# Total of three groups: sums in the off-diagonal quadrants, interleaved with the next group's scores, and copied in two halves

## The chip, the cores and the metric

The kernel runs on one core of a Trainium2 chip. The metric is the time of one execution in device microseconds (us); the kernel before took 373.97 us, the median of 3 runs (372.93 to 374.14). The times of single instructions below come from one profiled execution.

## The reference

For each of 4 batches and 8 heads, a state of 64x64 decays by a factor of its head at each of 768 steps and takes up one outer product; the output is the query times that state:

```python
for t in range(S):
    state = gamma * state + einsum('bhd,bhe->bhde', k[:, :, t], v[:, :, t])
    y[:, :, t] = scale * einsum('bhd,bhde->bhe', q[:, :, t], state)
```

The heads' outputs side by side are `x` (768 x 512 per batch), and go through a gated layer: `h = relu(x @ w_in)` is cut into `u` and `v`; `v` is normalised over its columns, multiplied by `w_spatial` over the steps, a bias is added, and `(u * v_s) @ w_out` is the output.

## The kernel before, in words

**Groups.** The steps of a batch are cut into 6 groups of 128 steps (24 groups in all), a group into two halves `i` of 64 steps. The 8 heads are 4 pairs `hp` of 2 heads `r`. The two heads of a pair lie in partitions 0 to 63 and 64 to 127; `place(hp, r)` says which (the order alternates with `hp`). Decay is taken out by scaling: values are multiplied beforehand (`scale_values`, "p"), outputs afterwards (`out_evict`, "E"), so the state is a plain running sum. For each half a head has three kinds of products of 64x64x64: its scores (keys times queries, `score`, "q"), masked on VectorE (`ret_mask`, "j"); its part of the state (`naturals` times `values`); and its outputs (`out_products`, "y"), which take the masked scores and the state before the half. Each of these float32 products is recorded as two matmuls, so a group has 32 for scores, 16 for each half's state, 32 for each half's outputs.

**Quadrants.** A product of 64x64 uses a quarter of TensorE's array: the input's partitions choose the rows, the output's partitions the columns. `score` reads and writes the same 64 partitions: diagonal quadrants.

**The state in the first groups.** Groups 0 to 5 (batch 0) run in an opening whose order is written out by hand in the string `START`; its words are a letter and a number, emitted in order, and each engine keeps that order. There the state is kept as one total in PSUM: `total_sum(g, i)`, word `t`, adds the half's products to the tile `total` (L301 to L314), in the diagonal quadrants. `total_copy(g, i)`, word `k`, has ScalarE copy the whole tile into the state that the next half's outputs read (L316 to L318). The next sum may not write before that copy has read. Eleven sums and copies are made, `t00` to `t50`.

**The other stages.** After the opening, `ret_set` (L340 to L375) interleaves scores of the next group with state products whose output goes to the other 64 partitions; there a copy or an addition per 64 partitions brings them back.

**Other words of `START` that the change passes.** `V` is the product of `x` with the `v` half of `w_in` (large matmuls of 128x128x512, three per word), `h` and `l` split a group's output `x` into a high and a low part (ScalarE, then GpSimd or VectorE), `a`, `c`, `H` and `R` split a weight from 64-bit words into high and low parts (ScalarE, VectorE, ScalarE, then GpSimd or VectorE), `r`, `s`, `w`, `n` and `N` normalise. `G` and `L` and `K` are loads on SyncE's queue: a group's keys and queries (`qk`, 3 buffers) and values (`vk`, 2 buffers), a weight, a part of `w_spatial`. A group's load waits until the outputs of the group three earlier are done.

**After the opening** the order of TensorE's work is written out too (`FIRST`, `REST`, `LAST`); the order on the other engines is made by the framework's own planner.

Of the kernel before, what the change touches and what calls it, by code (L numbers as in the profile page):

```python
# [21 lines left out]


START = (
# [10 lines left out]
)  # L35
FIRST = (
    "S6 W0 I4 W1 D1 X6 J9 S7 G9 D2 I5 X7 J10 G10 D3 W2 S8 W3 I6 X8 S9 V0 G11 W4 I7 X9 J11 S10 "
# [24 lines left out]
def tile_retention_gmlp(  # L62
# [12 lines left out]
    nc = tc.nc  # L75
    P = 128
    B = out.shape[0]
# [12 lines left out]
    ROWS = [slice(0, D), slice(D, P)]  # L90
# [27 lines left out]
    def keep(ins):  # L118

        if fixed:  # L120
            tc.keep_in_program_order(ins)

    def mm(out, lhs, rhs, start, stop, pin=False, shared=False):
        ins = nc.tensor.matmul(out, lhs, rhs, start=start, stop=stop, skip_group_check=shared)  # L124
        if pin or pinned or fixed:
            tc.keep_in_program_order(ins)
# [32 lines left out]
    def slot(n, dtype, name):  # L159

        cols = HALF // 2 if dtype == I64 else HALF
        return mpool.tile([P, HC, cols], dtype, tag=f"sp{n}", name=name, bufs=1)
# [5 lines left out]
    for n in ROOMS:  # L168
        t = slot(n, F32, f"room{n}").rearrange("p s c -> p (s c)")
# [85 lines left out]
    def place(hp, r):  # L255

        return ROWS[(r + hp) % 2]
# [40 lines left out]
    total = {}  # L298
    marks = {}

    def total_sum(g, i):  # L301
        if not total:
            total[0] = ps_o.tile([P, NP, D], F32, tag="o", name="total")
        for hp in range(NP):
            for r in range(2):
                rows = place(hp, r)
                mm(
                    total[0][rows, hp],
                    naturals[g][rows, i, hp],
                    values[g][rows, i, hp],  # L310
                    start=(g == 0 and i == 0 and hp == 0),
                    stop=True,
                    shared=True,
                )  # L314

    def total_copy(g, i):  # L316
        dst = states[g][:, 1] if i == 0 else states[g + 1][:, 0]
        keep(nc.scalar.copy(dst, total[0]))  # L318

    def score(g, i, hp, r, pin=False):  # L320
        rows = place(hp, r)
        ops = keys[g][rows, i, hp], queries[g][rows, i, hp]
        mm(marks[g][rows, i, hp], *ops, start=True, stop=True, pin=pin)

    def bank(name):
        return ps_r.tile([P, 2, NP, C], F32, tag="ret", name=name)
# [8 lines left out]
    def ret_mask(g):  # L335
        mk = mask_t[:, :].unsqueeze(1).broadcast_to([P, 2 * NP, C])
        s, d = (t.rearrange("p i h c -> p (i h) c") for t in (marks.pop(g), scores[g]))
        keep(nc.vector.tensor_tensor(d, s, mk, ALU.mult))
# [360 lines left out]
    def decay_copy():  # L699
# [17 lines left out]
        "q": lambda b, g, n: ret_scores(n),  # L717
        "p": lambda b, g, n: scale_values(n % 10, pick(n // 10)),
        "j": lambda b, g, n: ret_mask(n),
        "t": lambda b, g, n: total_sum(n // 10, n % 10),  # L720
        "k": lambda b, g, n: total_copy(n // 10, n % 10),
        "y": lambda b, g, n: out_products(n // 10, n % 10),
        "E": lambda b, g, n: out_evict(n),
# [114 lines left out]
```

## Time and profile before

| | us |
|---|---|
| median of 3 runs | 373.97 |
| the profiled execution's own time | 374.42 |
| its span in the trace | 372.7 |
| TensorE busy | 362.0 (97%) |
| VectorE busy | 237.2 (64%) |
| ScalarE busy | 155.1 (42%) |
| GpSimd busy | 135.5 (36%) |

The granted clock of TensorE is full (1.00) over the span. The span runs from the first to the last instruction; the execution's own time has 1.7 us around it. Engines are named PE (TensorE's matmuls), PEld (its weight loads), DVE (VectorE), ACT (ScalarE), POOL (GpSimd) and SP (SyncE). Matmuls are recorded with modelled ends and overlap, so a group's span is from its first start to the last one's end.

### The profile page before, as it was taken

How to read it: one execution, taken by the hardware profiler on the slowest of the kernel's cores; microseconds unless marked ns; L12 is line 12 of the kernel's file. 1: busy time of each engine (PE TensorE's matmuls, PEld its weight loads, DVE VectorE, ACT ScalarE, POOL GpSimd, SP SyncE). 2: the span in 40 equal slices, each digit the busy share in tenths (PEclk: the TensorE clock that was granted, in tenths of full speed). 3: DMA queues.
4: the chain of work that ended last, by engine and by line, in shares of the span. 5: the costliest groups of instructions: out<-in, count | busy, mean ns of one | idle time of the engine just before them, and what ended most of it. 6: DMA issues, size and time to landing. Idle time of an engine off the chain costs nothing.

```text
span 372.7 us, 10303 instructions
## 1 busy us (share of the span) xinstructions
PE 362.0 (97%) x4420; PEld 316.6 (85%) x4420; DVE 237.2 (64%) x514; ACT 155.1 (42%) x309; POOL 135.5 (36%) x137
## 2 busy tenths in 40 slices
PE   7798999999999999999999999999999999999995
PEld 3687785797998879999998888999998888999984
DVE  4989979995887866677674543376774433165530
ACT  3595781274334545533114445432323445432232
POOL 2254750001353523526424451327424341325041
PEclk9999999999999999999999999999999999999999
DMA  7997773001331731113305332021404002000022
GB/s 262 413 365 261 272 300 130 0 2 63 138 114 58 253 115 64 61 55 112 118 2 199 114 114 86 8 106 52 179 1 141 3 2 86 0 0 2 0 87 84
DMA packets 13153, 41.20 MB, mean 111 GB/s; under 512 B 1586, under 2 KB 1842, under 8 KB 13108
## 3 DMA queue, kind: packets, MB, share of 16 engines
q1 hardware_dynamic: 12964, 40.42, 29.8%
q8 instruction: 35, 0.57, 0.7%
q10 hardware_dynamic: 144, 0.13, 0.1%
q14 instruction: 10, 0.08, 0.1%
HBM read 34.25 MB, written 6.29 MB: 109 GB/s over the span
## 4 chain that ended last, share of the span: by engine, by line
PE 94%; DMA 2%; DVE 1%; issue 1%; ACT 0%; SPq 0%; POOL 0%; POOLq 0%; DVEq 0%
PE u L124 18%; PE v L124 18%; PE o L124 18%; PE y L124 10%; PE sp L124 8%; PE x L124 7%; PE z L124 5%; PE s L124 3%; PE d L124 3%; PE w L124 3%; DMA decay_t<-in_decay_dram 2%; PE total L124 1%; PE o_last L124 0%; SPq L129 0%; DVE xf L417 0%
## 5 line engine op out<-in xcount | busy, mean ns | idle before, releaser
L124 PE MATMUL u<-xh,winu_w 128*128 128x384 f32 x256 | 68.1, 338 | 0.0
L124 PE MATMUL v<-winv_w,xh 128*128 128x512 f32 x192 | 60.6, 397 | 0.0
L124 PE MATMUL o<-wout_w,gh 128*128 128x512 f32 (+1 forms) x192 | 60.4, 396 | 0.0
L124 PEld LDWEIGHTS u<-xh,winu_w 128*128 128x128 f32 x256 | 46.5, 188 | 0.8
L132 POOL TENSOR_TENSOR xl<-xf,xh 128x512 fp32r<-128x512 f32 x21 | 29.4, 1398 | 37.3 <-ACT xh L434 37.3
L124 PE MATMUL u<-xl,winu_w 128*128 128x384 f32 x128 | 42.9, 335 | 0.0
L124 PEld LDWEIGHTS v<-winv_w,xh 128*128 128x128 f32 x192 | 35.2, 188 | 7.8
L124 PE MATMUL y<-sp,a 128*128 128x384 f32 x216 | 41.6, 336 | 0.0
L124 PEld LDWEIGHTS o<-wout_w,gh 128*128 128x128 f32 x192 | 35.2, 188 | 7.3
L532 ACT CAST a<-vn 128x384 fp32r<-128x384 f32 x42 | 21.6, 514 | 46.0 <-PE y L124 16.9
L132 DVE TENSOR_TENSOR a<-vn,a 128x384 fp32r<-128x384 f32 x42 | 24.9, 593 | 24.6 <-ACT a L532 24.2
L132 POOL TENSOR_TENSOR gl<-ur,gh 128x384 fp32r<-128x384 f32 x24 | 26.8, 1116 | 37.4 <-ACT gh L628 37.0
L124 PEld LDWEIGHTS y<-sp,a 128*128 128x128 f32 x216 | 38.0, 188 | 0.2
L124 PE MATMUL v<-winv_w,xl 128*128 128x512 f32 x96 | 37.5, 390 | 0.0
L124 PE MATMUL o<-wout_w,gl 128*128 128x512 f32 (+1 forms) x96 | 37.3, 389 | 0.0
L475 DVE BATCH_NORM_STATS2 bst<-vr 128x6 f32<-128x512 f32 x24 | 16.6, 691 | 28.6 <-ACT vr L468 28.6
L417 DVE SCALAR_TENSOR_TENSOR xf<-x,decay_t,qd_t 128x128 f32<-128x128 f32 x96 | 27.1, 343 | 10.3 <-PE x L124 9.7
L482 POOL TENSOR_TENSOR rs<-rs,mhalf 128x1 f32<-128x1 f32 x24 | 13.5, 566 | 42.6 <-DVE rs L477 42.1
L124 PE MATMUL s<-qk 64*64 64x64 f32 x768 | 27.4, 221 | 0.1
L124 PEld LDWEIGHTS s<-qk 64*64 64x64 f32 x768 | 25.2, 137 | 2.1 <-issue 1.1
L498 ACT ACTIVATE vn<-vr,nb,rs 128x512 f32<-128x512 f32 x24 | 19.4, 814 | 17.8 <-DVE nb L487 16.8
L593 ACT ACTIVATE ur<-u 128x384 f32<-128x384 f32 x32 | 15.7, 490 | 26.8 <-PE u L124 26.6
(111 smaller groups left out, 671.7 us busy)
## 6 DMA issues: line engine op xcount, KB each, us to landing
qk<-in_groups_dram SPq DMA_DIRECT2D x24, 512.0 KB, 5.4
vk<-in_groups_dram SPq DMA_DIRECT2D x21, 512.0 KB, 4.8
out_dram<-ot SPq DMA_DIRECT2D x23, 256.0 KB, 2.9
wst<-in_w_sp_dram SPq DMA_DIRECT2D x4, 576.0 KB, 7.9
raw<-in_w_inv_dram SPq DMA_DIRECT2D x4, 512.0 KB, 7.3
raw<-in_w_inu_dram SPq DMA_DIRECT2D x4, 512.0 KB, 7.0
raw<-in_w_out_dram SPq DMA_DIRECT2D x4, 512.0 KB, 5.2
third<-in_groups_dram SPq DMA_DIRECT2D x3, 512.0 KB, 7.4
```

The source lines that it names most:

```text
L124: ins = nc.tensor.matmul(out, lhs, rhs, start=start, stop=stop, skip_group_check=shared)
L132: return eng.tensor_tensor(out, whole, high.bitcast(F32), ALU.subtract)
L417: nc.vector.scalar_tensor_tensor(xf[:, hp], t[hp % 2][:, hp // 2].rearrange("p i c -> p (i c)"), qg_t[:, c, hp : hp + 1], qd_t[:, hp], ALU ...
L475: keep(nc.vector.bn_stats(st, norm[b, c][0]))
L482: keep(nc.gpsimd.tensor_tensor(rs, rs, mhalf, ALU.pow))
L498: keep(nc.scalar.activation(vn[b][:, c], v, AF.Identity, bias=nb, scale=rs))
L532: nc.scalar.copy(t[:, 0], whole)
L593: keep(nc.scalar.activation(u, pu[:, :HALF], AF.Relu))
```

## The change

In the opening, the scores of groups 3, 4 and 5 are no longer a block of their own ahead of the sums (`q3`, `q4`, `q5`). `total_sum` of groups 2, 3 and 4 makes them: with `with_scores` each product of the sum follows one score of the next group, half `i` with half `i`. In `START` these sums have a 1 in front (`t120`, `t121`, `t130` and so on). All sums, also those without scores, now write to the other 64 partitions, so that `total` holds the pair's heads exchanged, and `total_copy` exchanges them back with two copies of 64 partitions. The masks of groups 4 and 5 move: `j4` from behind `h2` to behind `t131`, `j5` from behind `a4` to behind `t141`; `j3` keeps its place. The other words keep their order.

```diff
-    "h0 k01 c21 j1 t10 y10 a1 H2 k10 G3 c10 y11 p22 t11 c22 q2 c11 k11 c12 L3 l0 H1 q3 t20 k20 "
-    "E1 G4 R1 V00 j2 h1 t21 l11 p23 k21 y20 y21 L5 R2 j3 q4 t30 E2 a3 h2 j4 c30 V10 p24 V01 V11 "
-    "V02 L4 l12 c31 V20 a5 k30 y30 c32 t31 H3 k31 c50 G5 y31 q5 E3 t40 a4 j5 R3 V21 V12 k40 c40 "
-    "L6 c51 y40 p25 y41 t41 h3 l3 V03 a6 k41 c41 E4 c42 c52 r0 s0 G6 h4 l4 H4 V22 L8 R4 V13 V23 "
+    "E0 q1 h0 k01 c21 j1 t10 y10 a1 H2 k10 G3 c10 y11 p22 t11 c22 q2 c11 k11 c12 L3 l0 H1 "
+    "t120 k20 E1 G4 R1 V00 j2 h1 t121 l11 p23 k21 y20 y21 L5 R2 j3 t130 E2 a3 h2 c30 V10 p24 "
+    "V01 V11 V02 L4 l12 c31 V20 a5 k30 y30 c32 t131 j4 H3 k31 c50 G5 y31 E3 t140 a4 R3 V21 "
+    "V12 k40 c40 L6 c51 y40 p25 y41 t141 j5 h3 l3 V03 a6 k41 c41 E4 c42 c52 r0 s0 G6 h4 l4 H4 "
...
-    def total_sum(g, i):
+    def total_sum(g, i, with_scores=False):
         if not total:
             total[0] = ps_o.tile([P, NP, D], F32, tag="o", name="total")
+        if with_scores and i == 0:
+            marks[g + 1] = bank(f"s{g + 1}")
         for hp in range(NP):
             for r in range(2):
-                rows = place(hp, r)
+                if with_scores:
+                    score(g + 1, i, hp, r)
+                rows, other = place(hp, r), place(hp, 1 - r)
                 mm(
-                    total[0][rows, hp],
+                    total[0][other, hp],
...
     def total_copy(g, i):
         dst = states[g][:, 1] if i == 0 else states[g + 1][:, 0]
-        keep(nc.scalar.copy(dst, total[0]))
+        for r in range(2):
+            keep(nc.scalar.copy(dst[ROWS[r]], total[0][ROWS[1 - r]]))
...
-        "t": lambda b, g, n: total_sum(n // 10, n % 10),
+        "t": lambda b, g, n: total_sum(n // 10 % 10, n % 10, n >= 100),
```

## Rows read from the trace of the kernel before

**Rows 1.** The page's chain that ended last, by engine.
```profile
PE 94%; DMA 2%; DVE 1%; issue 1%; ACT 0%; SPq 0%; POOL 0%; POOLq 0%; DVEq 0%
```

**Rows 2.** Windows: stretch, its length, busy us and count of each engine, clock, DMA.
```profile
50.00:100.00 50.00, 50.00 (x381) 39.51 (x380) 42.07 (x84) 22.31 (x43) 5.69 (x6) 1.00 0.24 89
...
15.90:31.30 15.40, 13.89 (x381) 12.21 (x382) 13.76 (x26) 11.37 (x36) 8.39 (x6) 1.00 0.90 335
31.30:39.20 7.90, 7.18 (x126) 5.60 (x125) 7.79 (x19) 5.47 (x16) 2.09 (x2) 1.00 0.70 246
```

**Rows 3.** Timeline of PE: start, us, instruction, count, idle before and its releaser.
```profile
16.74 0.28 PE L124 MATMUL x<-ws,vk 64*64 64x64 f32 x3 [0.87 <-issue]
...
17.48 1.97 PE L124 MATMUL s<-qk 64*64 64x64 f32 x62
...
20.81 0.90 PE L124 MATMUL total<-third 64*64 64x64 f32 x15
...
23.46 0.63 PE L124 MATMUL total<-vk 64*64 64x64 f32 x15
...
31.82 0.33 PE L124 MATMUL total<-vk 64*64 64x64 f32 x3 [1.19 <-issue]
...
35.21 0.73 PE L124 MATMUL v<-winv_w,xh 128*128 128x512 f32 x2
...
39.39 0.28 PE L124 MATMUL x<-qk,third 64*64 64x64 f32 x4 [0.39 <-issue]
...
44.59 0.39 PE L124 MATMUL v<-winv_w,xl 128*128 128x512 f32 x1
```

**Rows 4.** DMA, 29.4 to 30.5 us: queue, packets, MB, share of 16 engines.
```profile
q8 instruction: 1, 0.02, 5.9%
```

**Rows 5.** DMA, 37.0 to 38.3 us.
```profile
q8 instruction: 1, 0.02, 5.3%
```

**Rows 6.** DMA, 31 to 37 us.
```profile
q1 hardware_dynamic: 480, 1.80, 87.0%
```

**Rows 7.** Timeline of SyncE's issues: start, us, what.
```profile
29.39 0.33 SPq L129 DMA_DIRECT2D qk<-in_groups_dram  x1
...
31.38 0.42 SPq L129 DMA_DIRECT2D wst<-in_w_sp_dram  x1
```

**Rows 8.** Line L124, 79.6 to 80.75 us: count, ns min/median/max, first and last start.
```profile
L124 PE MATMUL s<-qk x32: 218/218/267, 79.7 to 80.7; 64*64 64x64 f32 x32
...
L124 PE MATMUL d<-vk x32: 218/218/267, 79.8 to 80.7; 64*64 64x64 f32 x32
```

**Rows 9.** ScalarE's groups by form: count, busy us, mean ns, idle before.
```profile
L369 ACT COPY ws<-d 64x256 f32<-64x256 f32 x6 | 2.2, 367 | 0.6 <-PE d L124 0.6
```

**Rows 10.** Timeline of ScalarE.
```profile
18.83 0.35 ACT L318 COPY third<-total 128x256 f32<-128x256 f32 x1
...
20.03 0.37 ACT L318 COPY third<-total 128x256 f32<-128x256 f32 x1 [0.33 <-PE total L124]
...
22.75 0.35 ACT L318 COPY ws<-total 128x256 f32<-128x256 f32 x1
23.00 0.68 ACT L176 ACTIVATE room<-raw 128x512 f32<-128x512 f32 x1
...
28.93 0.37 ACT L318 COPY ws<-total 128x256 f32<-128x256 f32 x1 [0.92 <-PE total L124]
```

**Rows 11.** Timeline of VectorE.
```profile
34.43 0.43 DVE L197 TENSOR_SCALAR room<-df 128x512 int32<-128x512 int32 x1
...
35.49 1.41 DVE L197 TENSOR_SCALAR room<-df 128x512 int32<-128x512 int32 x1
...
41.47 1.12 DVE L417 SCALAR_TENSOR_TENSOR xf<-x,decay_t,qd_t 128x128 f32<-128x128 f32 x4 [0.32 <-PE x L124]
...
43.52 0.68 DVE L132 TENSOR_TENSOR xl<-xf,xh 128x512 fp32r<-128x512 f32 x1
```

**Rows 12.** Timeline of GpSimd.
```profile
35.06 1.55 POOL L132 TENSOR_TENSOR xl<-xf,xh 128x512 fp32r<-128x512 f32 x1 [3.98 <-ACT xh L434]
```

12 rows, old and new, of the table START are left out of this document.

## The prediction

> **What bounds the kernel now.** I began with the chain that ended last: TensorE holds 94% of it and DMA 2% [rows 1]. Then the busy time by stretch: from 50 to 100 us TensorE is busy for all 50.00 us [rows 2]. So whatever moves the moment at which TensorE leaves the opening (about 50 us, where the change lies) moves the end by as much, and nothing else does. Inside the opening TensorE is not full. I read its timeline for idle marked "issue", which means that it waited for nothing that the profile shows: 0.87 us before 16.74, 1.19 before 31.82 and 0.39 before 39.39 [rows 3]. Between the first two gaps lie 382 weight loads, between the last two 125 [rows 2]: that is three times 127, and 127 again. A gap after every 127th pair of weight load and matmul (the boundaries between pass with little or no gap) looks like the instruction stream itself, arriving in blocks. The DMA view says so too: in queue 8, "instruction", one packet of 0.02 MB is under way in 29.4 to 30.5 us [rows 4] and one in 37.0 to 38.3 us [rows 5], and TensorE goes on about 2.4 us after the start of each window, at 31.82 and 39.39. In the six microseconds before, 31 to 37, the load queue alone is listed, at 87.0% of all 16 DMA engines, and queue 8 moves nothing [rows 6]. The loads that fill this stretch were issued from 29.39 (qk6) to 31.38 (half of the spatial weights) [rows 7]. I read it so: the block that TensorE needs at 39 us is asked for when it takes up the block before, at 31.82, and is served behind the loads issued by then.
>
> The Trainium skill, "Runtime: NRT & Kernel Launch", section "Instruction fetch mechanics", says that the stream comes in blocks of 256 instructions of 16 KiB, fetched while the block before runs, and that the cost of crossing is mostly hidden. Size and count agree with rows 2, 4 and 5; the hiding does not, in this opening, where the three gaps add up to 2.45 us [rows 3]. By that rule the 2.0 us worked out below would pass on, as in the first rival.
>
> **The change part by part.** *Products interleaved.* A group's scores run at 1.97 us for 62 recorded matmuls, less 0.22 for the last one to drain: 28 to 29 ns each [rows 3]. Where scores and state products alternate between the diagonal and the other quadrants, as the later stages already do, 32 and 32 take 0.95 us from first to last start (79.7 to 80.7), 14.5 ns each [rows 8]. Each of the three groups has 32 score and 32 total matmuls, so 64 x 14.5 ns = 0.93 us is saved per group, 2.8 us in all, as far as TensorE is free to run them.
>
> *Copies in halves.* A copy of 64x256 takes 0.37 us on the mean [rows 9], and one of 128x256 0.35 to 0.37 us [rows 10], so a half costs what the whole did; the one after it starts 0.25 to 0.27 us later (22.75 to 23.00 [rows 10]). Eleven more copies are 2.9 us of ScalarE, and each total copy ends 0.26 us later.
>
> Now stage by stage, because most of both is hidden.
>
> To 16.74 us: the copies of groups 0 and 1 stand in the chain (the next sum may not overwrite the total before both halves have read it). Three of them follow one another before the gap, at most 0.8 us; the gap of 0.87 us [rows 3] hides it, since the block's packet waits for loads that are issued earlier and don't move. Without the gap it would cost the 0.8.
>
> Group 2 (17 to 22 us): the copy of the first total, k20, starts at 20.03 and ends at 20.40 [rows 10]. ScalarE can reach it at 18.83 + 2 x 0.26 + 0.52 (the cast behind k11) = 19.88, and its second half then ends at about 20.5. So t21 with scores starts at 20.55 instead of 20.81 [rows 3], gains 0.26 us at most, and runs into the end of a block in its 30th matmul of 32; the kernel before meets the same boundary in the 14th of its 16 there and ends it late (0.90 us for 15 matmuls [rows 3], against 0.63 at 29 ns). Gain 0.
>
> Group 3 (22 to 24 us): k21 starts at 22.75 and ends at 23.10 [rows 10], and the 0.93 us of scores hid that: t30 starts at 23.46 [rows 3]. Now the first score is followed by a product that must wait for both halves. With 0.12 us that ScalarE is behind, they end at about 23.50; t30 with scores runs to 24.0, where t30 ended. Gain 0, or a loss of 0.05.
>
> Group 4 (29 to 35 us): the same again with k31, which starts at 28.93 [rows 10]; the halves end at 29.56, so t40 with scores runs from 29.6 to 30.1. But now the boundary that cost 1.19 us falls elsewhere: the stream up to it is the same 382 pairs, but six large matmuls (V21, V12) and eight of y40 stand ahead of it. They take 1.5 us and fill the gap; TensorE reaches the boundary at 31.75 and goes on at 31.82 as before. Left are 88 small matmuls (24 of y40, 32 of y41, 32 of t41 with scores) x 14.5 ns = 1.28 us, so the next large ones start at 33.2 instead of 35.21 [rows 3]: 2.0 us ahead.
>
> The next block ends in y50, 125 pairs on, now at about 36.8. Its successor is asked for at 31.82 as before, behind the same loads (qk6 is issued when y31 ends, at most 0.1 us later), and comes at 37.1: TensorE goes on at 39.4 [rows 3, 5]. The 2.0 us become a gap of 2.6 us. I take this value, 0. The bounds: if the block came without waiting, the 2.0 us pass on; if it came later by what its request is later, the loss is that of the second rival.
>
> The Trainium skill, "DMA: Bandwidth & Descriptors", section "Queues, rings and completion order", says that a DMA engine takes turns between its queues packet by packet. Then the instruction packet would pass the waiting loads; rows 6 speak against it. By it the result is again the first rival.
>
> *VectorE.* The masks j4 and j5 move behind the later halves of their scores; both have time before y40 and y50. But VectorE is full here, and its plain tensor_scalar operations stall beside GpSimd: 1.41 us at 35.49 beside GpSimd's operation at 35.06 to 36.61 [rows 11, 12], where one alone takes 0.43 (34.43). Moved work changes which one meets it: I count one such stall lost and one gained, and 0.3 us of lateness from ScalarE's. There is room: VectorE waits 0.32 us for TensorE at 41.47, and the low part of group 5's output at 43.52 (0.68 us long, done at 44.20 [rows 11]) is wanted at 44.59 [rows 3], so 0.39 more. Cost 0 to 0.1; without that cover 0.3, and 1.0 for each further stall.
>
> Sum for the profiled execution: 0 + 0 (to 0.05) + 0 + 0 to 0.1, about +0.1 on its own 374.42 us (span 372.7 and 1.7 around it). It stands 0.45 above the median of 373.97, so I forecast 374.0.
>
> **The rivals.** *The fetch is not tied to the loads.* Then TensorE is 2.0 us ahead at 36.8. For it: the profile puts the gaps down to "issue" and names no load. Against it: rows 6. But the low part at 43.52 caps it: VectorE can be earlier by 0.32 and has 0.39 in hand, so 0.7 us, 373.3, no measurable change; only if VectorE also loses a stall (1.0 us) does 1.7 come through: 372.3.
> *All 2.8 us arrive*: 371.2. For it: the pace of rows 8. Against: the copies that the sums wait for in rows 10.
> *Slower: the fetch comes a fixed time after the boundary.* In the trace the block ends at 30.63 (31.82 less the idle 1.19) and the packet's window opens at 37.0. If that 6.4 us is the fetch's own time and not a queue of loads, the boundary now at 31.75 brings the packet at 38.1 and TensorE back at about 40.5, 1.1 to 1.35 us later: 375.3. It decides as soon as the boundary falls after 30.63, which it does. Against it: the packet of 29.4 [rows 4] came some 2.5 us after its boundary, which by the count of 127 lies in the large matmuls near 27 us.
> *VectorE meets two more stalls*: 0.3 + 2.0 - 0.7 = 1.6 us, 375.6.
>
> **How the numbers follow.** The forecast 0.56; the free fetch 0.16, of it 0.07 with no measurable change; all of the saving 0.06; the fixed fetch 0.15; VectorE's stalls 0.07. A measurement of this kernel can tell 0.3% (1.1 us) from no change. Faster 0.09 + 0.06 = 0.15, same 0.56 + 0.07 = 0.63, slower 0.22. The forecast's own range is 373.3 to 374.8. Left out below is the full saving (0.06), above the far part of the stalls; the range is 372.3 to 375.5.
>
> **What would show it.** Right: a TensorE gap of 2 us or more near 37 to 39.4 us and the restart within 0.2 us of 39.39; no gap near 31; the first large matmuls of 35.21 near 33.2; scores and total together at 14.5 ns. Wrong: the packet of 37.1 moved by more than 0.3 us, either way, or the low part of 43.52 arriving late with TensorE waiting for it. A time below 372.8 or above 375.1 would refute the forecast.

## The result and the profile after

The change makes the kernel slower: 376.76 us, the median of 7 runs (375.76 to 377.29), against 373.97. The ratio on record is 1.0067 (it is not the quotient of the two medians), with an interval of 1.0046 to 1.0088, so 1.7 to 3.3 us. The forecast was 374.0 with a range up to 375.5. The profiled execution took 376.83 us with a span of 375.1, 2.4 us longer than before. Of the experiment e1_halves below, one execution took 902.91 us and is left out.

TensorE holds 90% of the chain that ended last instead of 94% [rows 1]; VectorE and ScalarE have come in.

```profile
PE 90%; DMA 3%; DVE 3%; ACT 2%; issue 1%; SPq 0%; POOL 0%; POOLq 0%
```

By stretch (columns as in [rows 2]), TensorE is again full from 50 to 100 us, and the difference arises in the opening. A stretch at half the granted clock, 1.2 GHz, runs from about 17.7 to 21.1 us; the profiled execution before stood at 1.00 throughout, but 28 of 82 other executions of the kernel before have a mean granted clock of 0.990 to 0.995, so such stretches are not new with the change.

```profile
17.50:18.00 0.50, 0.44 (x10) 0.30 (x14) 0.50 (x2) 0.47 (x3) 0.00 (x0) 0.69 1.00 401
18.00:21.00 3.00, 3.00 (x86) 3.00 (x86) 2.77 (x8) 2.94 (x11) 0.00 (x0) 0.50 0.65 218
21.00:21.50 0.50, 0.50 (x29) 0.43 (x22) 0.50 (x1) 0.17 (x1) 0.26 (x1) 0.90 0.94 344
...
50.00:100.00 50.00, 50.00 (x381) 39.45 (x380) 42.03 (x86) 22.83 (x42) 7.10 (x8) 1.00 0.30 110
```

**The timeline of TensorE after.** It shows where the opening falls behind.

```profile
15.81 0.51 PE L124 MATMUL total<-vk 64*64 64x64 f32 x10 [3.08 <-issue]
...
25.72 0.27 PE L124 MATMUL total<-vk 64*64 64x64 f32 x1 [1.66 <-ACT ws L323]
...
26.34 0.73 PE L124 MATMUL v<-winv_w,xh 128*128 128x512 f32 x2
...
34.53 0.33 PE L124 MATMUL x<-ws,vk 64*64 64x64 f32 x4 [0.18 <-DVE xf L422]
...
36.70 0.73 PE L124 MATMUL v<-winv_w,xh 128*128 128x512 f32 x2
...
40.66 0.27 PE L124 MATMUL x<-third,third 64*64 64x64 f32 x2 [0.18 <-DVE xf L422]
...
43.52 0.72 PE L124 MATMUL v<-winv_w,xh 128*128 128x512 f32 x2
...
51.89 0.33 PE L124 MATMUL u<-xh,winu_w 128*128 128x384 f32 x1
```

The same points of the kernel before, to be set against these:

```profile
24.03 0.73 PE L124 MATMUL v<-winv_w,xh 128*128 128x512 f32 x2
...
41.28 0.73 PE L124 MATMUL v<-winv_w,xh 128*128 128x512 f32 x2
...
49.57 0.33 PE L124 MATMUL u<-xh,winu_w 128*128 128x384 f32 x1
```

The reader is to see three steps. TensorE is 26.34 - 24.03 = 2.31 us late when the large products of group 1 start. At V03, the next large products after group 4's sums (36.70, before 35.21 [rows 3]), it is only 1.49 late: 0.8 us have been won back, by products at the new pace and because the gap of 1.19 us before 31.82 [rows 3] is gone, less new waits of 0.39 us for `k31` and of 0.18 us twice for `E3`. At V30 (43.52 against 41.28) it is 2.24 late again, and that is carried to the end (51.89 against 49.57, +2.32). So something takes time before 26 us, and something else takes the gain back between 36 and 43 us. The lateness before 26 us need not reach the end: the experiment e6_early_half below is 1.42 us late at V10 (25.45) and 0.13 at the `u` products (49.70).

**Before 16 us.** ScalarE's timeline after:

```profile
10.12 0.76 ACT L323 COPY ws<-total 64x256 f32<-64x256 f32 x2 [0.36 <-PE total L124]
10.90 0.68 ACT L176 ACTIVATE room<-raw 128x512 f32<-128x512 f32 x1
14.32 0.62 ACT L439 CAST xh<-xf 128x512 fp32r<-128x512 f32 x1 [2.74 <-DVE xf L422]
14.97 0.74 ACT L323 COPY ws<-total 64x256 f32<-64x256 f32 x2
```

From the start of `k00` to the next instruction, `a2`, it is 0.78 us. A whole copy let the next one start 0.25 to 0.27 us after it [rows 10]. The two halves run one behind the other, 0.39 us each, and cost 0.51 us more instead of the 0.26 of the prediction. VectorE after:

```profile
11.62 0.43 DVE L182 TENSOR_SCALAR room<-room 128x512 f32<-128x512 f32 x1 [1.01 <-ACT room L176]
12.08 1.18 DVE L184 TENSOR_SCALAR room<-room 128x512 int32<-128x512 int32 x1
13.18 1.11 DVE L422 SCALAR_TENSOR_TENSOR xf<-x,decay_t,qd_t 128x128 f32<-128x128 f32 x4
```

and before:

```profile
11.12 0.43 DVE L182 TENSOR_SCALAR room<-room 128x512 f32<-128x512 f32 x1 [0.49 <-ACT room L176]
11.58 0.43 DVE L184 TENSOR_SCALAR room<-room 128x512 int32<-128x512 int32 x1
11.92 1.12 DVE L417 SCALAR_TENSOR_TENSOR xf<-x,decay_t,qd_t 128x128 f32<-128x128 f32 x4
```

Half a microsecond later, L184 runs into GpSimd's scaling of the values of group 1:

```profile
11.93 1.04 POOL L296 TENSOR_TENSOR vk<-vk,decay_t 128x512 f32<-128x512 f32 x1 [2.60 <-DMA vk<-in_groups_dram]
```

It takes 1.18 us instead of 0.43. The first eviction, `E0`, starts 1.26 us later (13.18 against 11.92), `h0` and behind it `k01` follow, and the sum that may not overwrite the total before `k01` has read it, `t10`, starts at 15.81 after 3.08 us of idle TensorE. `k01` ends at 15.71, yet the profile marks this idle time "issue"; the mark alone does not prove that an engine waits for its instructions. In the kernel before, `t10` started here:

```profile
14.07 0.68 PE L124 MATMUL total<-vk 64*64 64x64 f32 x16 [1.54 <-POOL vk L296]
```

The Trainium skill, "SBUF — State Buffer", section "Who interferes with whom", says that a tensor_scalar in a two-port mode and a GpSimd operation lock each other out for a whole instruction; the trace agrees (1.18 against 0.43 us), though it does not show the mode.

**Between 30 and 43 us.** VectorE after:

```profile
31.18 0.69 DVE L343 TENSOR_TENSOR ws<-s,mask_t 128x512 f32<-128x512 f32 x1 [1.12 <-PE total L124]
31.79 0.64 DVE L182 TENSOR_SCALAR room<-room 128x512 f32<-128x512 f32 x1
32.47 1.40 DVE L184 TENSOR_SCALAR room<-room 128x512 int32<-128x512 int32 x1
33.78 1.11 DVE L422 SCALAR_TENSOR_TENSOR xf<-x,decay_t,qd_t 128x128 f32<-128x128 f32 x4
...
39.40 1.12 DVE L422 SCALAR_TENSOR_TENSOR xf<-x,decay_t,qd_t 128x128 f32<-128x128 f32 x4
```

and before:

```profile
23.86 0.68 DVE L338 TENSOR_TENSOR ws<-s,mask_t 128x512 f32<-128x512 f32 x1
...
31.29 1.11 DVE L417 SCALAR_TENSOR_TENSOR xf<-x,decay_t,qd_t 128x128 f32<-128x128 f32 x4
...
36.82 1.11 DVE L417 SCALAR_TENSOR_TENSOR xf<-x,decay_t,qd_t 128x128 f32<-128x128 f32 x4
```

The mask `j4` ran at 23.86 without a wait. Now it stands behind `t131` and VectorE, full before, sits idle for 1.12 us until those scores are there. What is queued behind it, two operations on a weight (the second takes 1.40 us, beside GpSimd's operation of 32.23 to 33.58) and then the eviction `E3`, moves: `E3` starts at 33.78 (+2.49), `E4` at 39.40 (+2.58). TensorE's rows above name `xf L422` at 34.53 and 40.66: `y40` waits for `E3` and `y50` for `E4`, because a group's outputs take the two PSUM tiles that are left beside `total`, and the eviction of the group before frees them. And on ScalarE

```profile
40.55 0.62 ACT L439 CAST xh<-xf 128x512 fp32r<-128x512 f32 x1 [2.25 <-DVE xf L422]
...
42.21 0.76 ACT L323 COPY third<-total 64x256 f32<-64x256 f32 x2
```

`h4`, which waits 2.25 us for `E4`, holds up what stands behind it on ScalarE, and so `k50`, the copy that `y51` needs; then V30 follows, 2.24 us late. The forecast gap near 39.4 us is gone: TensorE has no idle marked "issue" from 26 to 44 us. In the DMA view of 38.2 to 39.0 us the instruction packet is there:

```profile
q8 instruction: 1, 0.02, 7.5%
```

In steps of 0.05 us it begins at 38.45, and before at 37.05 [rows 5]: 1.4 us later. TensorE goes on some 2.4 us behind such a packet (below), which would be about 40.85 here, and it gets there only then, at 40.88: the wait for `E4` hides the gap.

### The profile page after: what moved, and what is told of

Read it like the earlier page. It is cut to its first block, busy times and chain, and to the rows that moved or that the text cites. A ratio compares the mean times of both kernels' runs of the same rounds, so it can differ in the third digit from the quotient of the medians.

```text
span 375.1 us, 10314 instructions
## 1 busy us (share of the span) xinstructions
PE 362.2 (97%) x4420; PEld 316.1 (84%) x4420; DVE 236.8 (63%) x514; ACT 160.5 (43%) x320; POOL 134.8 (36%) x137
## 4 chain that ended last, share of the span: by engine, by line
PE 90%; DMA 3%; DVE 3%; ACT 2%; issue 1%; SPq 0%; POOL 0%; POOLq 0%
PE u L124 18%; PE o L124 18%; PE v L124 17%; PE y L124 10%; PE sp L124 8%; PE x L124 6%; PE z L124 5%; PE d L124 3%; PE s L124 2%; PE w L124 2%; DMA decay_t<-in_decay_dram 2%; DMA qk<-in_groups_dram 1%; PE total L124 1%; ACT ws L323 1%; DVE xf L422 1%
## 5 line engine op out<-in xcount | busy, mean ns | idle before, releaser
L124 PE MATMUL u<-xh,winu_w 128*128 128x384 f32 x256 | 68.2, 338 | 0.0
L124 PE MATMUL v<-winv_w,xh 128*128 128x512 f32 x192 | 60.6, 397 | 0.0
L124 PE MATMUL o<-wout_w,gh 128*128 128x512 f32 (+1 forms) x192 | 60.4, 396 | 0.0
L124 PEld LDWEIGHTS u<-xh,winu_w 128*128 128x128 f32 x256 | 46.5, 188 | 0.8
L132 POOL TENSOR_TENSOR xl<-xf,xh 128x512 fp32r<-128x512 f32 x21 | 29.0, 1381 | 39.4 <-ACT xh L439 39.4
L124 PE MATMUL u<-xl,winu_w 128*128 128x384 f32 x128 | 42.9, 335 | 0.0
L124 PE MATMUL y<-sp,a 128*128 128x384 f32 x216 | 41.6, 336 | 0.0
L124 PEld LDWEIGHTS v<-winv_w,xh 128*128 128x128 f32 x192 | 35.2, 188 | 7.6
L124 PEld LDWEIGHTS o<-wout_w,gh 128*128 128x128 f32 x192 | 35.2, 188 | 7.3
L124 PEld LDWEIGHTS y<-sp,a 128*128 128x128 f32 x216 | 38.1, 188 | 0.2
L124 PE MATMUL v<-winv_w,xl 128*128 128x512 f32 x96 | 37.5, 391 | 0.0
L124 PE MATMUL o<-wout_w,gl 128*128 128x512 f32 (+1 forms) x96 | 37.3, 389 | 0.0
L480 DVE BATCH_NORM_STATS2 bst<-vr 128x6 f32<-128x512 f32 x24 | 16.6, 691 | 28.7 <-ACT vr L473 28.7
L422 DVE SCALAR_TENSOR_TENSOR xf<-x,decay_t,qd_t 128x128 f32<-128x128 f32 x96 | 27.1, 342 | 9.4 <-PE x L124 9.4
L124 PE MATMUL s<-qk 64*64 64x64 f32 x768 | 29.5, 227 | 0.3 <-DMA qk<-in_groups_dram 0.3
L124 PEld LDWEIGHTS s<-qk 64*64 64x64 f32 x768 | 26.7, 141 | 2.6 <-issue 1.4
```

Of the source, the lines that this page charges most:

```text
L132: return eng.tensor_tensor(out, whole, high.bitcast(F32), ALU.subtract)
L422: nc.vector.scalar_tensor_tensor(xf[:, hp], t[hp % 2][:, hp // 2].rearrange("p i c -> p (i c)"), qg_t[:, c, hp : hp + 1], qd_t[:, hp], ALU ...
L480: keep(nc.vector.bn_stats(st, norm[b, c][0]))
```

## Experiments

Two theories stood after the traces. The early chain: the halves of the copies in groups 0 and 1, the stall that they run into, the idle TensorE and its clock (theory A). Its rival: the masks that moved behind the later halves of the sums. The first pair undoes one half of the change each.

**e1_halves**: the kernel before, its order kept, with off-diagonal sums and copies in halves.

```diff
-                rows = place(hp, r)
+                rows, other = place(hp, r), place(hp, 1 - r)
-                    total[0][rows, hp],
+                    total[0][other, hp],
-        keep(nc.scalar.copy(dst, total[0]))
+        for r in range(2):
+            keep(nc.scalar.copy(dst[ROWS[r]], total[0][ROWS[1 - r]]))
```

> The kernel before with one part of the change alone: all sums go to the other 64 partitions and each total is copied in two halves; order and score blocks (q3, q4, q5) stay. Theory A (the halves of the first two groups lie in the chain ScalarE copy - ScalarE split - VectorE - ScalarE copy, each half costs its full 0.38 us, VectorE then runs into GpSimd's operation of 12.1 us, TensorE idles some 3 us before t10 and its clock falls): the gap before t10 is about 3 us, the clock shows a half-speed stretch, and the time is 375.5 to 377. Theory B (the loss is the new order: sums with scores wait for the copies, mask j4 waits for t131): no more than 0.5 us over the kernel before, 374.0 to 374.5.

Measured 375.58 us, ratio 1.0029 (1.0015 to 1.0044). The halves alone, with nothing gained by interleaving, cost about 1.1 us. Only its times are used here.

**e2_interleave**: the kernel after with its new order, but sums on the diagonal and whole copies.

```diff
-                    total[0][other, hp],
+                    total[0][rows, hp],
-        for r in range(2):
-            keep(nc.scalar.copy(dst[ROWS[r]], total[0][ROWS[1 - r]]))
+        keep(nc.scalar.copy(dst, total[0]))
```

> The changed kernel without the exchange: scores alternate with the sums in the new order and the masks j4, j5 stand where the change puts them, but the sums stay in the diagonal quadrants and each total is copied whole. Theory A: the opening up to 17 us is as in the kernel before (t10 at 14.1 us, gap before 16.74, full clock), and the time is 373.5 to 374.5. Theory B: t130 waits for k21, j4 for t131, and VectorE's evictions come later: 375 to 376.5.

Measured 375.32, ratio 1.0027 (1.0012 to 1.0042). The new order costs about 1 us without any halves. The early chain is as before (`t10` at 14.03 us, the gap before 16.67 us 0.88 us long), and `j4` waits 2.34 us, `j5` 0.92:

```profile
30.98 0.69 DVE L342 TENSOR_TENSOR ws<-s,mask_t 128x512 f32<-128x512 f32 x1 [2.34 <-PE total L124]
...
36.64 0.69 DVE L342 TENSOR_TENSOR third<-s,mask_t 128x512 f32<-128x512 f32 x1 [0.92 <-PE total L124]
```

So both halves of the change lose, and neither theory alone will do. (The pace is not gained here: scores and sums share the diagonal.)

**e3_evict_first**: the kernel after with `E0` ahead of the weight's operations, so that the stall does not lie before it.

```diff
-... R20 G1 L1 p1 a2 G2 c20 E0 q1 h0 k01 ...
+... R20 G1 L1 p1 a2 G2 E0 c20 q1 h0 k01 ...
```

> The changed kernel with one swap in the opening's order: the eviction E0 stands ahead of the split c20 on VectorE, so E0 no longer waits behind an operation that waits for ScalarE and then stalls beside GpSimd. Theory A: E0 starts near 11.6 instead of 13.18 us, t10 near 14.3 instead of 15.8, no gap of 3 us, no half clock, and most of the 2.8 us comes back: 374 to 375. Theory B: the early stages are 1.5 us ahead but the later waits take it: 376 to 377.

Measured 376.79, ratio 1.0059 (1.0043 to 1.0075): no gain. `E0` started at 11.58 and `t10` at 14.23 us, as the edit meant, but VectorE did its delayed work afterwards and the mask `j1` was late in its turn. Part of the lead stayed (V10 at 25.77 against 26.34 after), until TensorE met a gap in `y50`:

```profile
14.23 0.68 PE L124 MATMUL total<-vk 64*64 64x64 f32 x16 [1.51 <-issue]
16.55 0.36 PE L124 MATMUL x<-ws,vk 64*64 64x64 f32 x8 [1.64 <-DVE ws L343]
...
42.22 0.28 PE L124 MATMUL x<-qk,third 64*64 64x64 f32 x4 [1.81 <-issue]
```

The instruction packet begins at 39.90 here. So this gap is of the kind that the prediction forecast, at the place that it forecast, and it makes V30 start at 44.11, 0.59 us later than after. The profiled execution is the slowest of the six (377.49); whether the others met the same gap is not known.

**e4_hold_clock**: the kernel after with eight matmuls ahead of `t10` that compute nothing, to keep TensorE at work in the idle stretch.

```diff
-... h0 k01 c21 j1 t10 y10 ...
+... h0 k01 c21 j1 x0 t10 y10 ...
+    def hold_clock():
+        wps = ps_m.tile([P, DM], F32, tag="m", name="hold")
+        for i in range(8):
+            mm(wps, wz[:, :P], wz, True, True)
```

> The changed kernel with eight matmuls of 128x512 (bf16 zeros, into a bank that nobody reads) ahead of t10, so that TensorE is not idle for 3 us there. They add 1.7 us of TensorE work inside the gap and leave all else. If the half clock after the gap (17.7 to 21.1 us) is part of the loss: the clock stays full, the stretch takes 1 to 1.7 us less, and the time falls by 0.5 to 1.5 us, to 375.2 to 376.3. If ScalarE's and VectorE's chain sets the pace there and the clock costs nothing: 376.8 as the changed kernel.

Measured 377.75, ratio 1.0082 (1.0059 to 1.0104). The idle time before `t10` fell from 3.08 to 1.26 us, yet the clock of the profiled execution fell to 0.52 between 17.6 and 21.0 us all the same. It did not do what it was made for, so it says nothing of what the clock costs; the median lies above both expected values.

**e6_early_half** and **e6_late_half**: the kernel before with one superfluous half copy behind each total copy, in groups 0 and 1 only, or from group 2 on only. The order and the sums are those of before.

```diff
         keep(nc.scalar.copy(dst, total[0]))
+        if g < 2:          # late: g >= 2
+            keep(nc.scalar.copy(dst[ROWS[0]], total[0][ROWS[0]]))
```

> The kernel before, diagonal sums and whole copies, with one redundant copy of 64 partitions after each of the four total copies of groups 0 and 1, and nothing else. If the halves' cost of 1.1 us comes from the chain of the first two groups: 375.0 to 375.8 (1.1 us over the kernel before). If it comes from the later copies: 374.0 to 374.6.

> The same with the redundant copies after the seven total copies of groups 2 to 5 alone. If the first two groups are the cause: 374.0 to 374.6, as the kernel before, since the score blocks hide the copies. If the later copies (above all that of t50 ahead of y51) are: 375.0 to 375.8.

Measured 374.76, ratio 1.0025 (1.0005 to 1.0045), early; 373.66, ratio 0.9985 (0.9970 to 1.0001), late. In the order of before the late copies are free; the early ones carry the price, though its interval nearly reaches zero. VectorE of the early one shows the same stall as the kernel after:

```profile
12.01 1.20 DVE L184 TENSOR_SCALAR room<-room 128x512 int32<-128x512 int32 x1
```

and its `t10` starts at 15.67 us, 2.72 us idle. These half copies are not quite those of the change. They stay in partitions 0 to 63, and the next instruction starts 0.27 us after one:

```profile
10.57 0.36 ACT L320 COPY ws<-total 64x256 f32<-64x256 f32 x1
10.84 0.68 ACT L176 ACTIVATE room<-raw 128x512 f32<-128x512 f32 x1
```

So one of them costs ScalarE 0.40 us (0.67 from the whole copy to the next instruction, instead of 0.27), and the halves of the change 0.51. The profiled execution of e6_early_half has a span of 372.9, no longer than before: the price shows in the median of 12 runs, and not in this trace.

**e5_fill**: the kernel after; work that VectorE has to do anyway is put ahead of the two waiting masks, `c50` ahead of `j4`, and `c41` with `a6` and `k41` ahead of `j5`.

```diff
-... c32 t131 j4 H3 k31 c50 G5 ... t141 j5 h3 l3 V03 a6 k41 c41 E4 ...
+... c32 c50 t131 j4 H3 k31 G5 ... t141 h3 l3 V03 a6 k41 c41 j5 E4 ...
```

> The changed kernel with two moves on VectorE: the split c50 goes ahead of the mask j4 and c41 ahead of j5, so that VectorE has work while it waits for t131 and t141 (it idles 1.12 us before j4 in the changed kernel). Theory C (the order's part of the loss is VectorE's idling before the late masks, which makes the evictions E3 and E4 late, and through E4, h4 and the copy of t50 TensorE's y51): E3 and E4 come about 1 us earlier, the large matmuls after y51 start near 42.5 instead of 43.5, and the time falls by about 1 us to 375.5 to 376. Theory A (only the delay of the first two groups counts): 376.5 to 377.

Measured 375.39, ratio 1.0039 (1.0026 to 1.0053), 1.4 us below the kernel after. Its VectorE:

```profile
30.42 0.43 DVE L184 TENSOR_SCALAR room<-room 128x512 int32<-128x512 int32 x1
...
31.33 0.69 DVE L343 TENSOR_TENSOR ws<-s,mask_t 128x512 f32<-128x512 f32 x1 [0.48 <-PE total L124]
31.94 1.12 DVE L422 SCALAR_TENSOR_TENSOR xf<-x,decay_t,qd_t 128x128 f32<-128x128 f32 x4
...
37.21 1.12 DVE L422 SCALAR_TENSOR_TENSOR xf<-x,decay_t,qd_t 128x128 f32<-128x128 f32 x4
```

`E3` is 1.84 and `E4` 2.19 us earlier than after, although `t10` (15.81) and `t130` (25.87) are as late as there. Of the 1.84 us, 0.64 are idle time before `j4` (0.48 against 1.12) and 0.97 the stall of L184, which now runs before GpSimd's operation (0.43 against 1.40). The place of the masks is one cause.

**e11_undo_group3**: the kernel after with group 4's scores in a block of their own again and `j4` back in its old place.

```diff
-... R2 j3 t130 E2 a3 h2 c30 ... c32 t131 j4 H3 ...
+... R2 j3 q4 t30 E2 a3 h2 j4 c30 ... c32 t31 H3 ...
```

> The changed kernel with the interleaving undone for group 3 alone: scores of group 4 are a block again ahead of t30, mask j4 stands behind h2 as before; groups 2 and 4 stay interleaved, all copies in halves. If the order's part is TensorE's wait of 1.66 us before t130 and VectorE's wait for t131: 375.3 to 376.0, about 1.2 us below the changed kernel. If each group's interleaving costs alike: 376.3.

Measured 375.86, ratio 1.0054 (1.0035 to 1.0072). `E3` came at 31.52, but `j5` still waited 0.64 us at 35.87, and `E4` started at 38.37, 1.16 us later than e5's. One mask in its old place is not enough: the later one pushes `E4` back by itself.

**e12_fill_k01, e13_both, e14_before_early, e15_early**: a test of both causes together. The early chain is loosened by ScalarE's order alone: `k01` ahead of `h0`, and `a2` ahead of `k00`.

```diff
 early moves:
-... t00 k00 y00 y01 t01 R20 G1 L1 p1 a2 G2 c20 E0 q1 h0 k01 ...
+... t00 a2 k00 y00 y01 t01 R20 G1 L1 p1 G2 c20 E0 q1 k01 h0 ...
 e12: after + e5's edit + k01 ahead of h0
 e13: after + e5's edit + both early moves
 e14: before + both early moves
 e15: after + both early moves
```

> The changed kernel with VectorE filled as in the run before (c50 ahead of j4, c41 ahead of j5), and the copy k01 ahead of the cast h0 on ScalarE, so that it no longer waits for the eviction E0. If two causes add (the halves in the first two groups' chain, 0.8 to 1.1 us; VectorE's waits at the late masks, 1.1 to 1.4 us) and k01 is the chain's main link: t10 starts near 13.3 instead of 15.8 us, and the time is 374.2 to 374.8. If the split a2 behind k00 carries the chain: t10 is early but y10 waits for the mask j1 (near 15.9), and 374.8 to 375.4 remains.

> The same, and the split a2 ahead of k00 on ScalarE, so that neither VectorE's c20 nor the mask j1 waits for the second half of k00. If the two causes are all: the opening to 17 us is as in the kernel before, and the time is that of the kernel before within 0.3 us, 373.7 to 374.3; lower only if the products' pace reaches the end. If a third cause is left, above 374.7.

> The control: the kernel before with the same two moves on ScalarE (a2 ahead of k00, k01 ahead of h0). The chain to 15.6 us is shorter, but the block of instructions that TensorE lacks until 16.74 us comes no earlier: 373.6 to 374.2, no change. If the early chain bounds the kernel before: 373.0.

> The changed kernel with the two moves on ScalarE alone, VectorE's order as the change has it. With causes that add: 375.2 to 375.9, a loss of 1.1 to 1.4 us left by the late masks. If the delay of the first two groups is what makes the masks late: 374.0 to 374.6.

| | masks as in after | masks behind other work |
|---|---|---|
| early chain as in after | after: 1.0067 (1.0046 to 1.0088) | e5: 1.0039 (1.0026 to 1.0053) |
| early moves | e15: 1.0033 (1.0010 to 1.0055) | e13: 0.9987 (0.9968 to 1.0006) |

The medians are 376.76, 375.39, 375.94 and 374.18 us. Against the median of the kernel before in the same round (373.97, 373.98, 374.21 and 374.21 us) they are 2.8, 1.4, 1.7 and 0.0 us longer. e12, with one of the two moves, took 374.54 (1.0003, 0.9983 to 1.0023). The same moves in the kernel before change nothing (e14: 374.24, ratio 0.9995, 0.9977 to 1.0014). Each remedy alone takes off roughly half of the loss, and both together all of it: two causes that add up. The early moves do not give `y10` its old place, since the mask `j1` stays late: 16.06 us in e12 and 15.69 in e13, against 16.11 after and 14.84 before. What comes earlier is ScalarE's work behind `k01`: `k10` starts at 16.10 in e12 against 16.95 after, `k11` at 18.95 against 19.78. TensorE of e13:

```profile
12.98 0.68 PE L124 MATMUL total<-vk 64*64 64x64 f32 x16 [0.24 <-POOL vk L296]
15.69 0.49 PE L124 MATMUL x<-ws,vk 64*64 64x64 f32 x8 [2.03 <-DVE ws L343]
24.53 0.27 PE L124 MATMUL total<-vk 64*64 64x64 f32 x1 [1.66 <-ACT ws L323]
31.02 0.27 PE L124 MATMUL total<-vk 64*64 64x64 f32 x1 [0.43 <-ACT ws L323]
...
38.75 0.28 PE L124 MATMUL x<-qk,third 64*64 64x64 f32 x4 [0.22 <-issue]
```

Even with both causes gone little of the 2.8 us of faster products comes out as time: in this trace TensorE starts the `u` products at 48.93 against 49.57 before, 0.64 us earlier, and the times don't tell that from nothing. TensorE spends the rest in waits: 2.03 us for the mask `j1` (VectorE meets GpSimd there after all), 1.66 and 0.43 us for the copies `k21` and `k31`, and a short gap again at a block boundary. No version was measurably faster than the kernel before.

## Why the prediction was wrong

**"So a half costs what the whole did; the one after it starts 0.25 to 0.27 us later": wrong by its size.** That distance was read from a whole copy [rows 10] and carried over to halves. The halves of the change don't overlap: 0.39 us each, 0.51 more per copy. The kernel before had shown it, in the form that the change adds, on the very line of [rows 9]:

```profile
81.17 0.74 ACT L369 COPY ws<-d 64x256 f32<-64x256 f32 x2
81.94 0.52 ACT L244 CAST sp<-wst 128x384 fp32r<-128x384 f32 x1
```

Two halves, and the next instruction 0.77 us after the first. These too exchange partitions (`dst[ROWS[r]]` from `ROWS[1 - r]`). A half copy that stays in its partitions does let the next instruction start after 0.27 us (e6_early_half), so what was missed is less likely the half than the exchange; no run tries halves without it. From the second group on, the prediction that ScalarE's added work costs nothing at the end held (e6_late_half), although single sums now wait for it (`t130` 1.66 us). The forecast for group 3, "Gain 0, or a loss of 0.05", fell with it: from V00 to V10 TensorE loses 0.78 us in e13 (20.25 and 25.15, before 19.91 and 24.03), and wins it back by V03 (34.79, before 35.21), where the gap before 31.82 is gone.

**"To 16.74 us ... at most 0.8 us; the gap of 0.87 us hides it": wrong, and this step holds one of the two causes.** It counted three copies and nothing else. But ScalarE and VectorE pass the work to each other here, and a shift of 0.5 us put L184 beside GpSimd's operation: +0.75 us. `t10` came 1.74 us later (15.81 against 14.07), twice the gap. The working priced such stalls only for the stretch around 35 us. The loss of this part, each run set against the kernel before of its own round, is 1.1 us by e15 (2.8 - 1.7), 1.4 by e13 (1.4 - 0.0) and 1.2 by e1. Whether the gap covers 0.8 us is not shown. e14 was to tell and does not: its `t10` starts 1.0 us earlier than before, but its mask `j1` is late, and `y10` starts at 15.62 instead of 14.84:

```profile
13.06 0.68 PE L124 MATMUL total<-vk 64*64 64x64 f32 x16 [0.61 <-POOL vk L296]
15.62 0.49 PE L124 MATMUL x<-ws,vk 64*64 64x64 f32 x8 [1.88 <-DVE ws L338]
```

**"The masks j4 and j5 ... both have time before y40 and y50": wrong, the other cause.** I asked when the mask is wanted, and not what is queued behind it. The working said that "VectorE is full here", and on a full engine that works in order a wait is handed on to all that is queued behind it: 1.12 us idle at `j4`, and the stall that the operations behind it met afterwards, put `E3` 1.84 us behind that of e5 with the same late TensorE. The price is 1.4 us by e5 (2.8 - 1.4), 1.7 by e13 (1.7 - 0.0), and 0.9 by e2, whose order alone is new.

**The forecast gap at 39.4 us: its kind is real, its time was wrong, and in the kernel after TensorE never got there early.** The working let TensorE reach `y40` at 31.6 us and `y50` at 36.8. Both need the tiles that `E3` (31.29 to 32.4 us before) and `E4` (36.82 to 37.9) free. With `E3` and `E4` at their old times the 2.0 us of lead could not have been reached, wherever the masks stand; the large products forecast for 33.2 started at 36.70, and in e13 at 34.79. The gap itself appears at this boundary in e13 (0.22 us, restart at 38.75), e12 (1.10, 39.65) and e3 (1.81, 42.22), and each time TensorE goes on 2.3 to 2.4 us after the instruction packet begins (36.45, 37.25, 39.90), as in the kernel before (37.05 and 39.39). So the reading of the gaps as blocks of instructions held. What failed is the packet's time: it moved to 38.45 in the kernel after, by 1.4 us, where the prediction named 0.3 us as a sign of being wrong. The loads moved as well: qk6 was issued at 31.68, 2.29 us later than in [rows 7], where the working had at most 0.1. That fits a packet that is served behind them, but does not prove it: from the issue of the last of these loads to the packet it is 5.7 us before, 4.4 in e13 and 7.2 in e3. (The view of [rows 6] also lists one packet of a second instruction queue, 14, at 0.3%, so the load queue was not quite alone.) What sets the packet's time stays open.

**What held.** Scores and sums together do run at the new pace: in TensorE's timeline after, the 32 matmuls of `t131` start from 30.48 to 30.90, some 14 ns apart. That hardly any of it reaches the end was right, in e13 even with both losses removed; but the forecast's reason, one gap of 2.6 us in the stream of instructions, is not what e13 shows (0.22 us there, and longer waits for VectorE and ScalarE). That e13's 374.2 lies so near the forecast 374.0 is in part luck.

**Of the rivals**, "VectorE meets two more stalls" came nearest in place and price (375.6), but the mechanism was another: the count of such stalls (a tensor_scalar of over 0.6 us) up to 43 us is five before and five after, one of them now at 12 us where it delays `E0`, and the rest is idle time. "The fetch comes a fixed time after the boundary" gave 375.3, but its gap does not appear in the kernel after, and the time is not fixed: 6.4 us before, and about 3.3 after, if by the prediction's count the boundary lies eight matmuls into `y40`, near 35.1 us (an estimate).

**Not settled** is the share of the clock, which the prediction left out. Of the 82 executions of the kernel before that ran beside the experiments, 54 with a mean granted clock of 0.997 or more have a median of 374.02 us, 21 at 0.993 to 0.995 one of 374.41, and 7 at 0.990 or 0.991 one of 375.92. Of the 7 runs after, the two at 0.998 took 375.76 and 375.93, the five at 0.990 to 0.995 took 376.40 to 377.29. So about 1.8 us of the loss stands at the full clock too, by two runs only, and up to 1 us goes with a lower clock, which is more frequent after (5 of 7 runs, against 28 of 82 before). It is frequent in the versions that change the stretch up to 17 us (12 of 12 runs in e5, 6 of 7 in e1, 7 of 12 in e6_early_half, 10 of 12 in e14) and less so in e2 (3 of 10) and e6_late_half (4 of 12), which leave it as it was, so the price of the early chain above may hold some of it. But 11 of e13's 12 runs stood at 0.989 to 0.995 with a median of 374.15. Whether the lower clock lengthens a run, or comes with what lengthens it, no run shows; e4 was meant to tell and did not.

## What to carry to other kernels

Before a wait is added on an engine without idle time, price what stands behind it in that engine's order, down to the buffer that this work frees; when the result of the waiting instruction is wanted is not enough. Read an added instruction's cost from its own form in the trace, its partitions in and out among them, with the start of the one after it, and not from a larger form nearby. A small shift in a chain across engines is priced at the shift plus every stall that it can newly meet, before a gap is called its cover.

## What was not expected of the hardware

ScalarE overlaps the end of one whole copy of 128x256 with the start of the next instruction by 0.10 us (0.37 us long, next start after 0.27), but not two copies of 64x256 that go to the other 64 partitions (0.76 us for the pair, next start after 0.78). A copy of 64x256 that stays in its partitions overlaps like a whole one (0.36 us long, next start after 0.27, in e6_early_half). The Trainium skill, "ScalarE: Activation LUTs", section "What ACT_TABLE_LOAD costs", gives about 93 ns of overlap for ACTIVATE instructions back to back; the trace agrees for the copies that stay in their partitions, and not for those that leave them. No run varies the exchange alone.

TensorE's granted clock fell to half for 3.4 us in the kernel after (17.7 to 21.1 us), after 3.08 us of idle TensorE. It fell in e2 too, from 16.7 to 20.1 us, behind no more idle time there than in the kernel before, whose clock stayed full (1.53 us ahead of `t10` and 0.88 us ahead of 16.67, against 1.54 and 0.87), and in e13 from 15.3 to 18.7 us. It fell in e6_late_half as well, from 16.6 to 20.1 us, a version that is no slower than the kernel before.

TensorE's gaps at the ends of instruction blocks ended 2.2 to 2.6 us after a packet of queue 8, "instruction", began, in all eleven traces that have one (0.16 to 1.81 us of idle TensorE). The idle time before `t10`, which the profile marks "issue" too, is not of this kind: in the kernel after the packet began at 14.40 and `t10` started at 15.81.
